# Layer 1 of a feed-forward block as Strassen block products, its weights streamed from scratch memory

## The chip, the cores and the metric

The kernel runs on one core of a Trainium2 chip. The metric is the device time of the whole program in microseconds. A core has five engines that run side by side and wait for one another through semaphores: TensorE (PE; its weight loads are shown as PEld), VectorE (DVE), ScalarE (ACT), GpSimd (POOL) and SyncE (SP), which here issues the transfers. PSUM is the memory that matmuls write; SBUF holds everything else on chip.

## The reference

For each of four batches a channel attention gives `x`, and a two-layer block follows:

```
qn = q / (norm of q over the tokens + 1e-6);  kn likewise            # [6080, 256]
s  = kn^T @ qn / tau                                                 # [256, 256]
a  = softmax of s over its last axis
x  = v @ a                                                           # [6080, 256]
h  = x @ w_in                                                        # [6080, 2048]
out = (max(h, 0) ** 2) @ w_out                                       # [6080, 256]
```

All inputs are float32, but the weights `w_in` (256 x 2048) and `w_out` (2048 x 256), which arrive as 64-bit floats and are decoded on chip. Four batches of 6080 tokens make 24320 rows.

## The kernel before

**Products in three terms.** Every float32 operand x of a large product is split into hi (x rounded to 12 significant bits) and lo = x - hi. A product is hi*hi + hi*lo + lo*hi, three matmuls that add up in one PSUM bank. ACT writes hi, DVE subtracts for lo.

**Folding.** (v a) w_in is computed as v (a w_in). For each batch, `fold` multiplies the softmax with a piece of `w_in` and leaves it in SBUF as the split pair `wph`, `wpl`, in four pieces of 512 feed-forward columns.

**Layer 1 and layer 2.** A batch is cut into 12 chunks of tokens, eleven of 512 and one of 448. A unit is one chunk and one tile of 128 feed-forward columns, so a chunk has 16 units. `layer1` (L287) does six matmuls into a bank `h` (two halves of the 256 channels, three terms each). ACT takes the Relu out of PSUM (`r`, L303) and squares it into `gh` (L306), DVE squares into `g` (L305) and subtracts for `gl` (L310). `layer2` (L316) follows two units later (`LAG`): six matmuls with the weights `woh` and `wol` into two banks `o`, which collect over the chunk's 16 units. Then ACT and DVE copy one bank each into `res`, which SP sends off.

**Side work.** Between the units of batch b the scores of batch b+1 are done: `score_load` (1 MB a load, four slots `kqt`), `score_norm` (ACT squares, DVE adds to `acc`), `score_split` (hi on ACT, lo on DVE), `score_mm` (six matmuls a tile of 128 rows, all 48 tiles into one bank of their own). After them follow the softmax (`norms`, `spread`, `exps`, `attnT`) and the folds for the next batch. `v` is loaded and split a chunk ahead (`load_v`, `split_v`).

**The start.** The first batch's scores come first, unsplit, while ACT and DVE take the norms; twelve tiles of the second batch follow as fill. The weights' 64-bit words are decoded by `decode_f64` (L65: four DVE and two ACT steps), piece by piece, the later ones among the units of the first two chunks, which share their pieces.

**Order.** Each step has a place in a list (`at(u, fn, ...)`: after unit u). Engines, slots and semaphores are the framework's: when the program is built, it arranges each engine's instructions by their place in the source and by when they are ready, so that an engine's order can differ from the source's. At run time each engine takes its instructions strictly in that built order.

Of the kernel before, what the change touches and what calls it, by code (L numbers as in the profile page):

```python
# [20 lines left out]
def tile_channel_attention_relu2_ffn(ctx, tc, kq, vT, tau, w_in, w_out, outT):  # L21
    """softmax over channels of normalised k^T q, then relu(x W_in)^2 W_out.

    Every float32 operand x of a large product is split exactly into hi = x rounded
    to 12 significant bits and lo = x - hi (float32r holds both), and
    hi*hi + lo*hi + hi*lo is accumulated in float32.  (v a) W_in is computed as
    v (a W_in).
    """
# [26 lines left out]
    win = const.tile([P, NH, DFF], F32, name="win")  # L55
    woh = const.tile([P, NJ, C], F32R, name="woh")
    wol = const.tile([P, NJ, C], F32R, name="wol")

    def h_bank():
        return ps_h.tile([P, CHUNK], F32, name="h", tag="h")  # L60

# [1 line left out]
    raws = {}  # L63

    def decode_f64(raw, W):  # L65
        """float64 words (low half first) to float32, rounded to nearest."""
        top = 122879.9921875
        shape = list(raw.shape[:3])
        hw = work.tile(shape, F32, name="hl", tag="hl", bufs=3)
        mag = work.tile(shape, F32, name="hl", tag="hl", bufs=3)  # L70
        low = work.tile(shape, I32, name="low", bufs=1)
# [10 lines left out]
    wiv = w_in.bitcast(U32).rearrange("(h p) f -> p h f", p=P)  # L82
    wov = w_out.bitcast(U32).rearrange("(j p) e -> p j e", p=P)

    def load_w_in(fc):
        raws["in", fc] = []
        for h, t in enumerate(("wph", "wpl")):
            raw = wpp.tile([P, FC, 2], U32, name=t, tag=t)
            nc.sync.dma_start(out=raw.rearrange("p n two -> p (n two)"),
                              in_=wiv[:, h, 2 * fc * FC:2 * (fc + 1) * FC])  # L90
            raws["in", fc].append(raw)

    def decode_w_in(fc):
        for h, raw in enumerate(raws.pop(("in", fc))):
            decode_f64(raw[:, None], win[:, h:h + 1, fc * FC:(fc + 1) * FC])

    def load_w_out(s):
        raw = work.tile([P, FPC, C, 2], U32, name="kqt", tag="kqt", bufs=KB)
        nc.sync.dma_start(out=raw.rearrange("p j n two -> p j (n two)"),
                          in_=wov[:, s * FPC:(s + 1) * FPC, :])  # L100
        raws["out", s] = raw

    def decode_w_out(s):
        js = slice(s * FPC, (s + 1) * FPC)
        W = work.tile([P, FPC, C], F32, name="sq", tag="sq")
        decode_f64(raws.pop(("out", s)), W)
        nc.scalar.copy(out=woh[:, js], in_=W)
        nc.vector.tensor_sub(out=wol[:, js], in0=W, in1=woh[:, js])  # L108

# [1 line left out]
    s_ps = {}  # L111
# [22 lines left out]
    def score_split(b, kt):  # L134
        x = kqt[b, kt // G][:, kt % G, :]
        hl = work.tile([P, 2, C2], F32R, name="hl", tag="hl", bufs=3)
        nc.scalar.copy(out=hl[:, 0], in_=x)  # L137
        nc.vector.tensor_sub(out=hl[:, 1], in0=x, in1=hl[:, 0])  # L138
        split[b, kt] = hl

    def score_mm(b, kt):
        if kt == 0:
            s_ps[b] = ps_s.tile([P, NH, C], F32, name="s")
        x = kqt[b, kt // G][:, kt % G, :]
        hl = split.pop((b, kt), None)
        for h in range(NH):
# [5 lines left out]
            for n, (l, r) in enumerate(terms):  # L152
                nc.tensor.matmul(out=s_ps[b][:, h, :], lhsT=l, rhs=r, start=kt == 0 and h == 0 and n == 0,  # L153
                                 stop=kt == NT - 1 and n == len(terms) - 1, skip_group_check=True)

# [34 lines left out]
    def spread(b):  # L190
        """the q norms' reciprocals, along the free axis of every partition."""
# [7 lines left out]
    def exps(b):  # L199
# [3 lines left out]
        for h in range(NH):  # L203
            e = small.tile([P, C], F32, name="e", bufs=2)
            nc.vector.scalar_tensor_tensor(out=e, in0=s_ps[b][:, h, :], scalar=z[:, h:h + 1],
# [23 lines left out]
    wp = {}  # L229
    wi = {}  # L230

    def fold_split(b, fc):
        wi[b, fc] = []
        for d in range(NH):
            w = work.tile([P, 2, FC], F32R, name="hl", tag="hl", bufs=3)
            x = win[:, d, fc * FC:(fc + 1) * FC]
            (nc.vector.tensor_copy if b else nc.scalar.copy)(out=w[:, 0], in_=x)
            nc.vector.tensor_sub(out=w[:, 1], in0=x, in1=w[:, 0])
            wi[b, fc].append(w)

    def fold(b, fc, ch):
# [21 lines left out]
    for b in range(B):  # L263
        for n0 in range(0, N, CHUNK):
            chunks.append((b, n0, min(CHUNK, N - n0)))
# [211 lines left out]
```

## Time and profile before

| | |
|---|---|
| runs of the kernel | 2286.97, 2287.17 and 2288.32 us; median 2287.17 us |
| the profiled execution, first to last instruction | 2286.2 us |
| matmuls in it | 10496 |

A profile is one execution. The page gives each engine's busy time and share of the span, the span in 40 slices (busy tenths, and GB/s that the transfers moved), and the chain of work that ended last, followed back from the last instruction. Then come groups of instructions: line, engine, operation, what is written and read with its shape, count, total busy time and mean duration in ns, and behind the second bar the idle time of the engine ahead of them with what ended it. A view by windows has, for each stretch, its length and then busy time and count of PE, PEld, DVE, ACT and POOL, the granted TensorE clock, the transfers' share and GB/s. A view in order of time gives start and length of each instruction in us. The row of a matmul is longer than the distance to the next, since matmuls overlap; their pace is read from starts.

### The profile page before, as it was taken

Reading aid. Unit: us, or ns where it says so; the run is one execution under the profiler, and the core shown is the slowest. Engines: PE = TensorE matmul, PEld = TensorE weight load, DVE = VectorE, ACT = ScalarE, POOL = GpSimd, SP = SyncE. Lnnn points to the kernel's source line nnn. Section 1 sums busy time; section 2 is a strip of 40 time slices with the busy share of each in tenths; the row PEclk is TensorE's granted clock in tenths of the full one; section 3 lists DMA queues with packets and bytes.
Section 4 is the critical chain, followed back from the end, with each engine's and each line's share of the span. In section 5 each row is a group of like instructions: output and inputs, shape, how many; then the busy total and the mean of one; then the engine's idle time right before and its main releaser. Section 6 shows DMA issues by size and latency. Waiting matters only on the chain.

```text
span 2286.2 us, 27309 instructions
## 1 busy us (share of the span) xinstructions
PE 2276.8 (100%) x10496; PEld 1913.3 (84%) x10496; DVE 1415.6 (62%) x2097; ACT 1246.0 (55%) x2033; POOL 0.8 (0%) x7
## 2 busy tenths in 40 slices
PE   9999999999999999999999999999999999999999
PEld 7788888888888888888888888888888888888888
DVE  7886656557656666655765666665566555555554
ACT  6885555546555555554654555555454445444444
POOL 0000000000000000000000000000000000000000
PEclk9999999999999999999999999999999999999999
DMA  9411111110011111111001111210001000000000
GB/s 350 156 56 56 37 38 65 47 42 32 19 36 56 56 37 56 55 56 55 19 20 53 37 56 38 74 37 19 18 19 36 19 19 29 28 19 24 31 10 18
DMA packets 37763, 110.29 MB, mean 48 GB/s; under 512 B 3456, under 2 KB 5504, under 8 KB 31616
## 3 DMA queue, kind: packets, MB, share of 16 engines
q1 hardware_dynamic: 37632, 108.54, 13.7%
q8 instruction: 82, 1.34, 0.2%
q14 instruction: 49, 0.40, 0.1%
HBM read 83.62 MB, written 24.90 MB: 47 GB/s over the span
## 4 chain that ended last, share of the span: by engine, by line
PE 98%; DMA 1%; DVE 1%; ACT 0%; issue 0%; SPq 0%; DVEq 0%
PE o L325 45%; PE h L296 45%; PE s L153 5%; PE h L253 2%; DMA kqt<-kq 1%; DMA v<-vT 0%; DVE acc L132 0%; PE h L169 0%; ACT sq L131 0%; DVE vl L282 0%; DVE low L78 0%; SPq L120 0%; PE h L220 0%; PE h L194 0%; ACT L175 0%
## 5 line engine op out<-in xcount | busy, mean ns | idle before, releaser
L305 DVE TENSOR_TENSOR g<-r 128x512 f32<-128x512 f32 (+1 forms) x752 | 515.9, 686 | 660.8 <-ACT r L303 660.4
L303 ACT ACTIVATE r<-h 128x512 f32<-128x512 f32 (+1 forms) x768 | 455.5, 593 | 860.2 <-PE h L296 856.0
L296 PE MATMUL h<-vh,wph 128*128 128x512 f32 (+1 forms) x1536 | 597.7, 389 | 0.0
L296 PE MATMUL h<-vl,wph 128*128 128x512 f32 (+1 forms) x1536 | 596.3, 388 | 0.0
L325 PE MATMUL o<-gh,woh 128*128 128x512 f32 (+1 forms) x1536 | 594.8, 387 | 0.8 <-ACT gh L309 0.8
L325 PE MATMUL o<-gl,woh 128*128 128x512 f32 (+1 forms) x1536 | 594.6, 387 | 0.5 <-DVE gl L310 0.5
L296 PE MATMUL h<-vh,wpl 128*128 128x512 f32 (+1 forms) x1536 | 594.7, 387 | 0.0
L325 PE MATMUL o<-gh,wol 128*128 128x512 f32 (+1 forms) x1536 | 594.6, 387 | 0.0
L310 DVE TENSOR_TENSOR gl<-g,gh 128x512 fp32r<-128x512 f32 (+1 forms) x768 | 527.0, 686 | 90.5 <-ACT gh L309 6.3
L306 ACT ACTIVATE gh<-r 128x512 fp32r<-128x512 f32 (+1 forms) x752 | 472.4, 628 | 21.6
L325 PEld LDWEIGHTS o<-gh,woh 128*128 128x128 f32 x1536 | 288.3, 188 | 58.6 <-ACT gh L309 1.3
L296 PEld LDWEIGHTS h<-vh,wpl 128*128 128x128 f32 x1536 | 288.4, 188 | 58.3 <-DVE wpl L258 0.4
L325 PEld LDWEIGHTS o<-gl,woh 128*128 128x128 f32 x1536 | 288.2, 188 | 58.1 <-DVE gl L310 1.2
L325 PEld LDWEIGHTS o<-gh,wol 128*128 128x128 f32 x1536 | 288.3, 188 | 57.1 <-DVE wol L108 0.3
L296 PEld LDWEIGHTS h<-vh,wph 128*128 128x128 f32 x1536 | 288.9, 188 | 53.3 <-DVE wpl L258 0.2
L296 PEld LDWEIGHTS h<-vl,wph 128*128 128x128 f32 x1536 | 288.9, 188 | 52.3
L132 DVE TENSOR_TENSOR acc<-acc,sq 128x1024 f32<-128x1024 f32 x92 | 112.4, 1222 | 29.5 <-ACT sq L131 26.1
L137 ACT CAST hl<-kqt 128x512 fp32r<-128x512 f32 x132 | 81.7, 619 | 77.1 <-PE s L153 75.3
L138 DVE TENSOR_TENSOR hl<-kqt,hl 128x512 fp32r<-128x512 f32 x132 | 91.1, 690 | 51.7 <-ACT hl L137 51.7
L153 PEld LDWEIGHTS s<-hl 128*128 128x128 f32 x792 | 112.4, 190 | 10.3
L153 PE MATMUL s<-hl 128*128 128x256 f32 x792 | 115.6, 282 | 0.0
L131 ACT ACTIVATE sq<-kqt 128x1024 f32<-128x1024 f32 x92 | 96.4, 1055 | 25.4 <-DMA kqt<-kq 21.0
(69 smaller groups left out, 614.3 us busy)
## 6 DMA issues: line engine op xcount, KB each, us to landing
kqt<-kq SPq DMA_DIRECT2D x47, 1024.0 KB, 4.8
v<-vT SPq DMA_DIRECT2D x44, 512.0 KB, 3.7
outT<-res SPq DMA_DIRECT2D x88, 256.0 KB, 2.0
kqt<-w_out SPq DMA_DIRECT2D x4, 1024.0 KB, 9.6
wph<-w_in SPq DMA_DIRECT2D x4, 512.0 KB, 9.4
wpl<-w_in SPq DMA_DIRECT2D x4, 512.0 KB, 10.0
v<-vT SPq DMA_DIRECT2D x4, 448.0 KB, 3.5
outT<-res SPq DMA_DIRECT2D x8, 224.0 KB, 1.9
```

Of the source, the lines that this page charges most:

```text
L131: nc.scalar.activation(out=sq, in_=x, func=AF.Square)
L132: nc.vector.tensor_add(out=accs[b], in0=accs[b], in1=sq)
L137: nc.scalar.copy(out=hl[:, 0], in_=x)
L138: nc.vector.tensor_sub(out=hl[:, 1], in0=x, in1=hl[:, 0])
L153: nc.tensor.matmul(out=s_ps[b][:, h, :], lhsT=l, rhs=r, start=kt == 0 and h == 0 and n == 0, stop=kt == NT - 1 and n == len(terms) - 1, sk ...
L253: nc.tensor.matmul(out=ps, lhsT=l[:, d, cs], rhs=wi[b, fc][d][:, r, :], start=n == 0, stop=n == 3 * NH - 1)
L296: nc.tensor.matmul(out=ps[:, :T], lhsT=l[:, ch, cs], rhs=r[:, ch, :T], start=n == 0, stop=n == 3 * NH - 1)
L303: nc.scalar.activation(out=r[:, :T], in_=ps[:, :T], func=AF.Relu)
L305: nc.vector.tensor_mul(out=g[:, :T], in0=r[:, :T], in1=r[:, :T])
L306: nc.scalar.activation(out=gh[:, :T], in_=r[:, :T], func=AF.Square)
L310: nc.vector.tensor_sub(out=gl[:, :T], in0=g[:, :T], in1=gh[:, :T])
L325: nc.tensor.matmul(out=o[:, :T], lhsT=l[:, j, es], rhs=r[:, :T], start=j == 0 and n == 0, stop=j == NJ - 1 and n == 2)
```

## The change

**Seven products for eight.** Two feed-forward tiles (f = 1, 2; tile j and tile j + 8) and two halves of a chunk of up to 1024 tokens (n = 1, 2) make a quad. Its layer 1 is a product of 2 x 2 blocks (the channels' halves are the inner blocks), and Strassen's scheme in Winograd's form takes seven block products of three terms for eight. `A11, A12, A22, S2, S3, S1, S4` are the weights' blocks and combinations. A batch has six chunks, five with halves of 512 tokens and one with halves of 480, and eight quads a chunk: 192 quads in all.

**The seven products** (m1 to m7) end in four blocks "11", "21", "22", "12". TensorE adds to a bank that already holds a sum, so some sums are copied by ACT from bank to bank (m1's from B to X, then S2's is added to B and copied to Z); m7 is copied to SBUF, and DVE adds it to B and Z out of PSUM (`plus_m7`). Each of the two banks `h` is used for B and m7 in turn, and for score pairs and folds. X and Z have one bank each, and layer 2 has four.

**The weights.** `combine` makes S1 to S4 from the folded weights, splits all seven and writes them to scratch memory in DRAM (128 x 2 x 7 x 128 words of 4 bytes, 917,504 bytes for one j). `load_wt` brings them back for every quad of every chunk but the first, into three slots. The decoded `w_in` goes to scratch too and is loaded again for each batch.

**Who does what.** The subtractions for the low parts of score tiles, of v's combinations (from the second chunk on) and of the later batches' weights move to or are added on POOL, as are the combinations themselves; for the first batch and the first chunk they run on DVE. Scores are gathered in pairs of tiles in an `h` bank and added to `s_acc` in SBUF by DVE (`score_burst`, `score_add`); score loads are 0.5 MB. At the start, the first piece of `w_in` is decoded behind the scores, `decode_w_out` stands ahead of the first quad, and the three later groups are prepared during the first chunk.

```diff
-    def layer1(ci, j):
...
-        for ch in range(NH):
-            for l, r in ((wh, vh), (wh, vl), (wl, vh)):
-                nc.tensor.matmul(out=ps[:, :T], lhsT=l[:, ch, cs], rhs=r[:, ch, :T],
...
+    def combine(b, g):
+        eng = nc.gpsimd if b else nc.vector
+        u = us.pop((b, g))
+        S = work.tile([P, 4, GW], F32, name="sq", tag="sq")
+        s2, s3, s1, s4 = (S[:, i] for i in range(4))
+        eng.tensor_add(out=s1, in0=u[:, 0, 1], in1=u[:, 1, 1])
+        eng.tensor_sub(out=s2, in0=s1, in1=u[:, 0, 0])
+        eng.tensor_sub(out=s3, in0=u[:, 0, 0], in1=u[:, 0, 1])
+        eng.tensor_sub(out=s4, in0=u[:, 1, 0], in1=s2)
+        for i in range(2):
+            j = 2 * g + i
+            w = work.tile([P, 2, NP, P], F32R, name="wt" if b == 0 else "wc", bufs=WB if b == 0 else 1)
+            js = slice(i * P, (i + 1) * P)
+            for o, x in ((w[:, :, 0:2], u[:, :, 0, js]), (w[:, :, 2:3], u[:, 1:2, 1, js]), (w[:, :, 3:7], S[:, :, js])):
+                nc.scalar.copy(out=o[:, 0], in_=x)
+                eng.tensor_sub(out=o[:, 1], in0=x, in1=o[:, 0])
+            wsc[b, j] = scratch.tile([P, 2, NP, P], F32, name=f"wsc{j}", bufs=2)
+            nc.sync.dma_start(out=wsc[b, j], in_=w.bitcast(F32))
...
+    def load_wt(ci, j):
+        wt[ci, j] = work.tile([P, 2, NP, P], F32R, name="wt", bufs=WB)
+        nc.sync.dma_start(out=wt[ci, j].bitcast(F32), in_=wsc[chunks[ci][0], j])
...
+    def v_combos(ci):
+        eng = nc.gpsimd if ci else nc.vector
...
+        t1 = diff(b12, b11)
+        t2 = diff(b22, t1)
+        for i, x in ((A11, lambda: b11), (S2, lambda: t2), (A12, lambda: b21), (S3, lambda: diff(b22, b12)),
+                     (A22, lambda: diff(b21, t2)), (S1, lambda: t1), (S4, lambda: b22)):
+            yield ci, i, x
+    def v_split(ci, i, x):
...
+        nc.scalar.copy(out=t[:, 0, :T], in_=x)
+        (nc.gpsimd if ci else nc.vector).tensor_sub(out=t[:, 1, :T], in0=x, in1=t[:, 0, :T])
...
+    def product(q, i, out, start):
+        ci, j = q
+        T = chunks[ci][2]
+        w, v = wt[ci, j], vt[ci, i]
+        for n, (l, r) in enumerate(((0, 0), (0, 1), (1, 0))):
+            nc.tensor.matmul(out=out[:, :T], lhsT=w[:, l, i], rhs=v[:, r, :T], start=start and n == 0,
+                             stop=n == 2, skip_group_check=True)
...
+    def block(q, c, ps=None, s=None):
...
+        if ps is not None:
+            nc.scalar.activation(out=r[:, :T], in_=ps[:, :T], func=AF.Relu)
+            nc.scalar.activation(out=gh[:, :T], in_=r[:, :T], func=AF.Square)
             nc.vector.tensor_mul(out=g[:, :T], in0=r[:, :T], in1=r[:, :T])
         else:
+            nc.vector.scalar_tensor_tensor(out=g[:, :T], in0=s[:, :T], scalar=0.0, op0=ALU.max,
+                                           in1=s[:, :T], op1=ALU.mult)
             nc.scalar.copy(out=gh[:, :T], in_=g[:, :T])
         nc.vector.tensor_sub(out=gl[:, :T], in0=g[:, :T], in1=gh[:, :T])
...
+    def m1(q):
+        st["B"] = h_bank()
+        product(q, A11, st["B"], True)
+        st["X"] = ps_x.tile([P, HMAX], F32, name="x")
+        nc.scalar.copy(out=st["X"][:, :T], in_=st["B"][:, :T])
+    def m6(q):
+        product(q, S2, st["B"], False)
+        st["Z"] = ps_z.tile([P, HMAX], F32, name="z")
+        nc.scalar.copy(out=st["Z"][:, :T], in_=st["B"][:, :T])
+    def m2(q):
+        product(q, A12, state[q]["X"], False)
+        block(q, "11", ps=state[q]["X"])
+    def m7(q):
+        H = h_bank()
+        product(q, S3, H, True)
+        nc.scalar.copy(out=state[q]["m7"][:, :T], in_=H[:, :T])
+    def m4(q):
+        product(q, A22, state[q]["B"], False)
+        state[q]["21"] = plus_m7(q, state[q]["B"])
+    def m5(q):
+        product(q, S1, state[q]["Z"], False)
+        state[q]["22"] = plus_m7(q, state[q]["Z"])
+        block(q, "21", s=state[q]["21"])
+        block(q, "22", s=state[q]["22"])
+    def m3(q):
+        product(q, S4, state[q]["Z"], False)
+        block(q, "12", ps=state[q]["Z"])
...
+    plan = (m1, ("11", 0), ("11", 1), ("21", 0), m6, m2, ("21", 1), m7, ("22", 0), m4, m5, ("22", 1), ("12", 0),
+            ("12", 1), m3)
...
+    def score_burst(b, kts):
+        s = h_bank()
+        for kt in kts:
+            score_mm(b, kt, s, kt == kts[0], kt == kts[-1])
+        score_add(b, s)
...
-    G = 4
+    G = 2
     KB = 4
-    EARLY = 3
+    HB = 3
+    TB = 3
+    WB = 3
+    VB = 8
+    GB = 5
+    EARLY = 6
...
+    decode_w_in(0)
+    early_mm(early[:4])
+    spread(0)
+    exps(0, s0)
+    fold_split(0, 0)
+    early_mm(early[4:8])
+    attnT(0)
+    for step in v_combos(0):
+        v_split(*step)
+    load_v(1)
+    early_mm(early[8:])
+    score_add(1, s1)
+    fold(0, 0, 0, ps_z.tile([P, HMAX], F32, name="z"))
+    fold(0, 0, 1)
+    decode_w_out(0, 0)
+    decode_w_out(0, 1)
+    combine(0, 0)
```

In `plan`, a name is a step of layer 1 of the current quad, and a pair ("21", 0) the three matmuls of layer 2 for that block of the quad before and one half of the output channels. Each step and each pair is three matmuls, 45 in a quad. `at(n - 1.5, load_wt, ci, j)` asks for a quad's weights one and a half quads ahead; `combine` of the next batch stands in the last seven quads of a batch, 1.4 quads apart.

More of the change, by code (lines that the diff above doesn't have):

```diff
@@ L80, in decode_f64 @@
                                        op0=ALU.bitwise_and, in1=low.bitcast(U32), op1=ALU.bitwise_or)
[L82 to L108, printed above, removed]
@@ L111, in tile_channel_attention_relu2_ffn, with load_w_in @@
-    s_ps = {}
+    wiv = w_in.bitcast(U32).rearrange("(h p) (t f) -> p h t f", p=P, t=2)
+    wov = w_out.bitcast(U32).rearrange("(t g j p) e -> p g t j e", p=P, t=2, j=2)
+    win = {}
+    def load_w_in(g):
+        raws["in", g] = []
+        for h in range(NH):
+            raw = work.tile([P, 2, GW, 2], U32, name="kqt", tag="kqt", bufs=KB)
+            nc.sync.dma_start(out=raw.rearrange("p t n two -> p t (n two)"),
+                              in_=wiv[:, h, :, 2 * g * GW:2 * (g + 1) * GW])
+            raws["in", g].append(raw)
@@ L269, in load_v @@
+    def load_wt(ci, j):
+        wt[ci, j] = work.tile([P, 2, NP, P], F32R, name="wt", bufs=WB)
+        nc.sync.dma_start(out=wt[ci, j].bitcast(F32), in_=wsc[chunks[ci][0], j])
+    widths = [min(HMAX, (N - n0) // 2) for n0 in range(0, N, 2 * HMAX)]
+    assert sum(widths) * 2 == N and all(w % 2 == 0 for w in widths)
+    chunks = [(b, 2 * sum(widths[:i]), w) for b in range(B) for i, w in enumerate(widths)]
+    NCH = len(widths)
+    raw_v = {}
+    vt = {}
     def load_v(ci):
         b, n0, T = chunks[ci]
-        v = work.tile([P, NH, CHUNK], F32, name="v", bufs=1)
@@ new lines, in plus_m7 @@
+    def plus_m7(q, ps):
+        T = chunks[q[0]][2]
+        s = work.tile([P, HMAX], F32, name="s", bufs=2)
+        nc.vector.tensor_add(out=s[:, :T], in0=ps[:, :T], in1=state[q]["m7"][:, :T])
+        return s
+    def m4(q):
[6 more added lines that the diff above has]
+        block(q, "22", s=state[q]["22"])
@@ new lines, in layer2 @@
+        o = outs[n, e]
+        wg, wj = j // 2, 2 * f + j % 2
+        es = slice(e * P, (e + 1) * P)
+        for k, (l, r) in enumerate(((woh, gh), (wol, gh), (woh, gl))):
+            nc.tensor.matmul(out=o[:, :T], lhsT=l[:, wg, wj, es], rhs=r[:, :T],
+                             start=first and k == 0, stop=last and k == 2)
+        if last:
+            res = work.tile([P, HMAX], F32, name="res", bufs=3)
+            (nc.vector.tensor_copy if e else nc.scalar.copy)(out=res[:, :T], in_=o[:, :T])
+            nc.sync.dma_start(out=ov[:, e, b * N + n0 + n * T:b * N + n0 + (n + 1) * T], in_=res[:, :T])
@@ L427, in tile_channel_attention_relu2_ffn @@
[L427 to L448 removed]
+        pairs = list(range(k0, NT, 2))
@@ new lines, in tile_channel_attention_relu2_ffn @@
+        end = when[pairs[-1]]
+        at(end + 0.6, score_burst, b, [NT - 2, NT - 1])
+        at(end + 0.8, norms, b)
+        at(end + 1.2, spread, b)
+        at(end + 1.3, lambda b=b: exps(b, s_acc[b]))
+        at(end + 1.9, attnT, b)
+        for g in range(NG):
+            u = u0 + QB - NJ + 1.0 + 1.4 * g
+            at(u - 1.5, load_win, b, g)
+            at(u - 0.3, fold_split, b, g)
+            at(u, fold, b, g, 0)
+            at(u + 0.4, fold, b, g, 1)
+            at(u + 0.5, combine, b, g)
@@ new lines, in tile_channel_attention_relu2_ffn, with start, run_side @@
+    for n, (ci, j) in enumerate(quads):
+        if ci:
+            at(n - 1.5, load_wt, ci, j)
+        if j == 0 and ci:
+            if ci > 1:
+                at(n - NJ + 2.05, load_v, ci)
+            def start(ci=ci, n=n):
+                for k, step in enumerate(v_combos(ci)):
+                    at(n + (-1.2, -0.95, -0.9, -0.6, -0.5, -0.4, -0.25)[k], v_split, *step)
+            at(n - 2.0, start)
+    def run_side(t):
+        while True:
+            due = sorted(u for u in side if u <= t)
+            if not due:
+                return
+            u = due[0]
+            todo = side.pop(u)
+            for fn, args in todo:
+                fn(*args)
```

350 lines of the change are left out of this document (172 added, 178 removed).

## The prediction

> **What bounds the kernel now.** I read the page's shares of the span and the transfer rates of its 40 slices first, then the chain that ended last, then the matmuls in order of time.
>
> ```profile
> span 2286.2 us, 27309 instructions
> ...
> PE 2276.8 (100%) x10496; PEld 1913.3 (84%) x10496; DVE 1415.6 (62%) x2097; ACT 1246.0 (55%) x2033; POOL 0.8 (0%) x7
> ...
> GB/s 350 156 56 56 37 38 65 47 42 32 19 36 56 56 37 56 55 56 55 19 20 53 37 56 38 74 37 19 18 19 36 19 19 29 28 19 24 31 10 18
> ...
> PE 98%; DMA 1%; DVE 1%; ACT 0%; issue 0%; SPq 0%; DVEq 0%
> ```
>
> TensorE is busy over all of the span, and 98% of the chain that ended last is TensorE. A busy share alone could hide pauses, because a row of a matmul is longer than its step; so I take the step from the starts of equal instructions twelve matmuls apart, for both chunk widths:
>
> ```profile
> 1899.75 0.39 PE L325 MATMUL o<-gh,wol 128*128 128x512 f32 x1
> 1902.47 0.39 PE L325 MATMUL o<-gh,wol 128*128 128x512 f32 x1
> ...
> 2259.65 0.36 PE L325 MATMUL o<-gh,wol 128*128 128x448 f32 x1
> 2262.08 0.36 PE L325 MATMUL o<-gh,wol 128*128 128x448 f32 x1
> ```
>
> At 512 columns twelve take 2.72 us, 0.2267 us each; at 448 they take 2.43 us, 0.2025 each. Twelve is exactly one unit (six of layer 1, six of layer 2), so in this stage nothing but the number of matmuls counts. 704 units of 2.72 and 64 of 2.43 us are 2070 us of the 2286: a change pays here if it removes matmuls and lets nothing else end last.
>
> **The matmuls removed.** Four units (two feed-forward tiles, two halves) have 24 matmuls of layer 1; seven products of three have 21. Layer 2 keeps its 24, so a quad has 45 matmuls for 48. The new chunks are five of 512 and one of 480 per batch and half, 8 quads each: 160 quads of 512, 32 of 480. Between the two measured steps, 480 columns take 0.2146 us. 160 x 45 x 0.2267 + 32 x 45 x 0.2146 = 1632 + 309 = 1941 us. **This removes 129 us.** Score, fold and early-score matmuls keep their numbers.
>
> **What the other engines get.** Their durations, one shape a row:
>
> ```profile
> L310 DVE TENSOR_TENSOR gl<-g,gh 128x512 fp32r<-128x512 f32 x704 | 487.0, 692 | 82.3 <-ACT gh L309 6.3 <-PE o L325 1.5 <-ACT gh L306 0.9
> L306 ACT ACTIVATE gh<-r 128x512 fp32r<-128x512 f32 x688 | 435.4, 633 | 19.6
> L303 ACT ACTIVATE r<-h 128x512 f32<-128x512 f32 x704 | 420.6, 597 | 801.2 <-PE h L296 799.7 <-DVE gl L310 1.5
> L132 DVE TENSOR_TENSOR acc<-acc,sq 128x1024 f32<-128x1024 f32 x92 | 112.4, 1222 | 29.5 <-ACT sq L131 26.1 <-ACT acc L128 0.5
> L131 ACT ACTIVATE sq<-kqt 128x1024 f32<-128x1024 f32 x92 | 96.4, 1055 | 25.4 <-DMA kqt<-kq 21.0 <-DVE acc L132 4.2
> L137 ACT CAST hl<-kqt 128x512 fp32r<-128x512 f32 x132 | 81.7, 619 | 77.1 <-PE s L153 75.3 <-PE h L253 1.5 <-DVE low L78 0.3
> L282 DVE TENSOR_TENSOR vl<-v,vh 128x512 fp32r<-128x512 f32 x88 | 60.2, 685 | 0.3 <-ACT vh L281 0.3
> L329 DVE COPY res<-o 128x512 f32<-128x512 f32 x44 | 30.1, 684 | 0.0
> L329 ACT COPY res<-o 128x512 f32<-128x512 f32 x44 | 25.1, 570 | 0.0
> masks.py:199 POOL TENSOR_SCALAR_AFFINE_SELECT ident<-ident 128x128 f32<-128x128 f32 x1 | 0.3, 294 | 0.0
> ```
>
> Per quad ACT does three copies out of PSUM (0.57), two Relu (0.60), two squares (0.63) and two casts (0.62): 5.4 us. DVE does two additions of m7, four g and four gl: ten of 0.69, 6.9 us. A quad takes TensorE 10.2 us, so both fit. About 0.65 score pairs fall on each quad of the score stage. A pair costs DVE 1.22 for the norm and 0.68 for the new addition out of PSUM, since scores now leave their bank after every pair, and ACT 1.06 + 2 x 0.62. That makes DVE 8.2 and ACT 7.0 us a quad. The pair's 12 matmuls widen the quad too. Their step comes from two rows of the chain, three units and one score tile of six matmuls apart:
>
> ```profile
> 872.04 1.39 PE h L296 x6
> 880.94 1.39 PE h L296 x6
> ```
>
> 8.90 - 3 x 2.72 = 0.74 us for six, so 0.65 x 1.48 = 1.0 us: 11.2 us a quad with scores.
>
> POOL, which does seven small things in the kernel before, gets the low parts of the score tiles, all of v's combinations from the second chunk on, and the later batches' weight combinations. Before has no POOL operation with two inputs. Below, I bound one of 512 elements by DVE's 0.69; above, by four times POOL's own row of 128 elements, 1.18. I take 1.18, the same engine. Per batch that is 48 + 66 + 8 subtractions of 512, 144 us, and about 26 us in `combine`: 170 us beside a TensorE stage of 531 us (40 quads of 10.2, eight of 9.66, 24 pairs of 1.48, 48 fold matmuls). POOL alone is no bound.
>
> **Steady waits.** A quad has new hand-overs: the copy X lies between m1 and m2, 12 matmuls or 2.72 us apart; Z likewise. From the end of m4 to the start of m3 there are also 2.72 us, in which DVE reads both banks, 2 x 0.69; 1.3 us are spare. A norm addition of 1.22 in front just fits; with the score addition too, m3 is 0.6 us late. A pair also takes one of the two `h` banks for its 1.48 us and the 0.68 of the addition; from m7's copy to the next m7 one is free for some 38 matmuls, 8.6 us, so that I cost at nothing. m3's lateness, over 66 pairs, is 40 us if it always happens and nothing if never. The order on an engine isn't the source's: the cast of v, written after the softmax, ran at 52.20, ahead of zq's copy:
>
> ```profile
> 52.20 1.12 ACT L281 CAST vh<-v 128x512 fp32r<-128x512 f32 x2
> ...
> 53.23 0.36 ACT L196 COPY zq<-h 128x256 f32<-128x256 f32 x1
> ```
>
> So work that isn't ready lets other work pass when the program is built, and I take less than half, **plus 22 us** with the folds' evictions. `combine` with its one `wc` buffer makes the second copies on ACT wait for POOL and a DMA; by the same ordering I cost that at nothing (18 us, 12 times 1.5, if a Z copy is stuck behind it).
>
> **The start.** Here the cover goes.
>
> ```profile
> 45.31 0.69 DVE L166 TENSOR_TENSOR acc<-acc 128x512 f32<-128x512 f32 x1
> ...
> 61.37 0.50 PE L296 MATMUL h<-vh,wph 128*128 128x512 f32 x1
> ...
> 64.47 3.18 PE L153 MATMUL s<-kqt 128*128 128x256 f32 x14
> ```
>
> ```profile
> L238 DVE TENSOR_TENSOR hl<-win,hl 128x512 fp32r<-128x512 f32 x32 | 22.0, 688 | 0.5
> L78 DVE CUSTOM_DVE_ANT_0 low<-hl,low 128x1024 uint16<-128x1024 uint16 x8 | 5.5, 687 | 0.6 <-ACT low L75 0.4
> L79 DVE SCALAR_TENSOR_TENSOR win<-hl,low 128x512 uint32<-128x512 uint32 x8 | 5.5, 685 | 0.0
> L205 DVE SCALAR_TENSOR_TENSOR e<-s,z,zq 128x256 f32<-128x256 f32 x8 | 3.7, 478 | 0.1
> L77 DVE TENSOR_SCALAR hl<-hl 128x512 int32<-128x512 int32 x8 | 3.4, 421 | 0.0
> L72 DVE TENSOR_SCALAR hl<-wph 128x512 f32<-128x512 f32 x4 | 1.7, 426 | 0.9 <-PE h L253 0.9
> ```
>
> Before, layer 1 begins at 61.4 with 3.2 us of early scores still to come. Afterwards DVE must do ahead of the first product, from about 45.3 us on: decoding the first w_in and w_out pieces (four halves of 0.43 + 0.42 + 0.69 + 0.69, 8.9), v's first chunk (four differences, seven low parts: 7.5), five norm additions (6.1), the softmax (about 5: the 0.69 of L166, two of 0.48, and small steps that I estimate at 3), the fold's low parts and aTl (2.1), the score copy (0.7) and combine up to its first tile (four of 0.45 and three of 0.3 to 0.7, about 3.2). That is 33 us, to about 78. The score loads, now of 0.5 MB with four in flight, cost nothing: by the last row above, 14 early matmuls take 3.2 us, so the eight of one load take 1.8, and three other loads cover 5.4 us (a load of twice the size landed in 4.8, quoted below); if they don't, some 3 us come on top. TensorE's own work there would end near 67. I take 77: **plus 12 us** against 64.6 (3 to 17).
>
> In the first chunk, weights are prepared for three more groups. Before, that stage had DVE at 87% and ACT at 86% (85.3 and 84.3 of 98.6 us), TensorE at 97.3 us, its clock granted in full (1.00):
>
> ```profile
> 61.37:160.00 98.63, 97.33 (x425) 79.31 (x425) 85.34 (x123) 84.34 (x135) 0.00 (x0) 1.00 0.27 95
> ```
>
> Now TensorE needs 8 x 10.2 + 36 fold matmuls = 90 us; DVE 8 x 6.9 + 3 x (8.9 decode, 1.4, 4.6 combine) + 1.4 = 101 us, and the steps hang on each other and on loads. I take **plus 16 us** (11 from the sums, 30 if v's and w_out's 17 POOL operations hold DVE up).
>
> **Streamed weights.** 184 loads and 32 stores of 0.92 MB, 198 MB, are 90 GB/s over the span. The slices above carry 10 to 156 after the first, which ran at 350.
>
> ```profile
> kqt<-kq SPq DMA_DIRECT2D x47, 1024.0 KB, 4.8
> ```
>
> A slightly larger load landed in 4.8 us; the weights are asked for 1.5 quads, 15 us, ahead. Cost: nothing, while SP isn't held by a full `kqt` ring.
>
> **Sum**, against the profiled execution: 2286.2 - 129 + 12 + 16 + 22 = 2207. The runs' median lies 1.0 us above that span: **2208 us**.
>
> **The rivals.** 1. **DVE and POOL don't run side by side.** Seven POOL operations at the start can't show this. If a POOL subtraction and a DVE operation with two inputs in SBUF exclude each other, what decides is DVE plus POOL per stage: 331 (quads) + 29 + 16 + 17 (norms, score additions, rest) + 170 = 563 us beside TensorE's 531, worst in the eight fold quads, where combine piles up. Never overlapping, three batches lose 32 us each: 2208 + 96 = 2304, slower than before. It needs 84 of those 96 us to be slower by over 0.2%; DVE's reads of PSUM and its idle time should hide a part, so half, 2256, is this rival's own middle. For it: at 1.18 us DVE and POOL exceed the stage. Against it: at 0.69 POOL shrinks to about 100 us, and the sum to 493. The Trainium skill, "SBUF — State Buffer", section "Who interferes with whom", says that a DVE instruction with two SBUF inputs contends with a GpSimd instruction that reads SBUF, and elsewhere on that page that the loser blocks for the whole instruction; by that rule this rival holds in full, and no run here shows it yet.
> 2. **TensorE waits at the hand-overs in every quad with scores**, 0.6 us or more on 109 quads, and combine blocks ACT: 2186 + 65 + 18 = 2269. For it: one X and one Z bank. Against: the spare 1.3 us.
> 3. **Everything is hidden**: no steady wait, the start at its lower bounds: 2286 - 129 + 3 + 11 + 1 = 2172.
> 4. **The weights come late** behind blocked loads on SP, 0.5 us a quad: 2208 + 92 = 2300. Against it: the 15 us of lead.
>
> **How the numbers follow.** Forecast 0.55 (2178 to 2235), rival 1 0.25 (0.09 of it slower, 0.03 the same), rival 2 0.10, rival 3 0.06, rival 4 0.04 (half slower). Faster 0.85, same 0.04, slower 0.11; 0.2%, 4.6 us, is about what a measurement tells from no change. From 2178 to 2292 about 0.17 is left out.
>
> **What would show it.** Right: 4032 layer-1 matmuls of unchanged step; the first product near 77 us; the second chunk begun near 182; TensorE's busy time short of the span by some 50 us, most of it before 190. Rival 1: DVE rows of 128x512 clearly above 692 ns wherever POOL is busy, and TensorE gaps released by DVE in the last eight quads of a batch. Rival 2: gaps ahead of m2, m3 and m5 released by ACT or DVE at unchanged durations. Rival 4: gaps released by DMA. The forecast fails if POOL's subtraction is far from 1.18 us, or if the start runs past 200 us.

## The result and the profile after

| | us |
|---|---|
| before, 4 runs | 2286.62 to 2288.32, median 2287.07 |
| after, 4 runs | 2416.30 to 2426.01, median 2421.07 |
| ratio | 1.0585, 95% interval 1.057 to 1.060 |
| the profiled execution after, span | 2419.3 |

The changed kernel is 134 us slower where the prediction had it 79 us faster; 2421 lies outside its range. The page after, first its shares:

```profile
span 2419.3 us, 27297 instructions
...
PE 2243.9 (93%) x9920; PEld 1827.8 (76%) x9920; DVE 1696.8 (70%) x2343; ACT 1361.5 (56%) x2389; POOL 722.7 (30%) x544
...
wt<-wsc SPq DMA_DIRECT2D x184, 896.0 KB, 4.6
```

The matmuls that were to go are gone, 10496 - 9920 = 576, and the streamed weights land in 4.6 us. But TensorE, busy for all of the span before, now has 175 us in which it does nothing, and POOL went from 0.8 to 723 us. Where the pauses lie is seen in the first chunk of the last batch, which has no side work beside it. The view by windows (length, then busy time and count of PE, PEld, DVE, ACT and POOL, granted clock, transfers' share, GB/s), first for the chunk's first quad, then for its other seven:

```profile
1895.60:1911.40 15.80, 11.94 (x46) 9.32 (x45) 9.76 (x12) 7.51 (x15) 10.74 (x7) 0.89 0.43 156
1911.40:1982.80 71.40, 71.40 (x316) 59.14 (x315) 47.92 (x72) 39.02 (x68) 6.23 (x6) 1.00 0.29 97
```

Seven quads take 10.20 us each with TensorE busy throughout, exactly the predicted pace. The first takes 15.8, and in it POOL works for 10.7 us: on the last three low parts of this chunk's `v` and, once the next `v` has landed, on the first four operations for that. The clock granted in it is 0.89: behind TensorE's pause of 3.31 us three matmuls take 1.45 us from start to start, where three took 0.70 ahead of it, so the pause costs speed after it as well. So it goes at every chunk between the first and the last: by the starts of their first products, first quads take 12.7 to 20.6 us, where a quad takes 10.2, or 11.7 with a score pair. The last chunk's first quad takes 10.3; no `v` follows it, and POOL works for 4.3 us in it.

The groups by shape show the second sign. DVE and POOL after:

```profile
L387 DVE TENSOR_TENSOR gl<-g,gh 128x512 fp32r<-128x512 f32 x640 | 493.7, 790 | 74.6 <-ACT gh L386 21.9 <-ACT gh L381 12.8 <-ACT x L396 0.5
L382 DVE TENSOR_TENSOR g<-r 128x512 f32<-128x512 f32 x320 | 268.4, 839 | 313.2 <-ACT r L380 309.1
L419 DVE TENSOR_TENSOR s<-h,m 128x512 f32<-128x512 f32 x160 | 110.0, 687 | 66.4 <-PE h L369 53.9 <-ACT m L414 12.3 <-issue 0.2
L150 POOL TENSOR_TENSOR hl<-kqt,hl 128x512 fp32r<-128x512 f32 x132 | 184.0, 1413 | 718.1 <-ACT hl L149 703.0 <-DVE gl L387 14.9
L357 POOL TENSOR_TENSOR vt<-tt,vt 128x512 fp32r<-128x512 f32 x76 | 124.8, 1653 | 369.7 <-ACT vt L356 369.5
```

DVE's operations with two inputs in SBUF take 790 and 839 ns on average (692 before), the addition that reads PSUM on one side (L419) takes 687, as it does without POOL in experiment 3, and POOL needs 1.41 to 1.65 us for what I had taken at 1.18. One boundary in order of time (start, length, instruction, in brackets the idle time before it and what ended it):

```profile
1985.67 1.74 POOL L357 TENSOR_TENSOR vt<-v,vt 128x512 fp32r<-128x512 f32 x1
1986.18 1.78 DVE L382 TENSOR_TENSOR g<-r 128x512 f32<-128x512 f32 x1
...
1987.44 0.33 SPq L328 DMA_DIRECT2D v<-vT  x1
...
1991.29 0.62 ACT L356 CAST vt<-v 128x512 fp32r<-128x512 f32 x1 [5.29 <-DMA v<-vT]
...
1992.29 0.59 ACT L403 COPY z<-h 128x512 f32<-128x512 f32 x1
...
1992.93 0.98 PE L369 MATMUL h<-vt,wt 128*128 128x512 f32 x3 [3.19 <-ACT z L403]
```

POOL's last low part ends at 1987.41, and only then can `v`, which has one buffer, be loaded again. ACT's first cast of the next `v` waits for that load, and the copy of Z, which TensorE waits for, stands behind the cast in ACT's order. TensorE's largest waits in the whole kernel (us in total, times, longest) are these:

```profile
PE h L369 <- ACT x L396: 51.5, 34, 6.7
PE h L369 <- ACT z L403: 51.0, 21, 3.5
PE z L369 <- DVE s L419: 18.8, 18, 3.0
PE o L454 <- DVE gl L387: 14.9, 20, 3.2
```

By these, 102 us end with ACT's copies of X and Z and 34 us with DVE. So two explanations offer themselves: an **order** on ACT that makes TensorE wait for a load (and, more generally, a chain POOL, load, ACT, TensorE), and the **ports**: DVE and POOL hold each other up, rival 1 of the prediction. The experiments are to part them.

### The profile page after: what moved, and what is told of

The parts are those of the page before. It is cut to its first block, busy times and chain, and to the rows that moved or that the text cites. A ratio compares the mean times of both kernels' runs of the same rounds, so it can differ in the third digit from the quotient of the medians.

```text
span 2419.3 us, 27297 instructions
## 1 busy us (share of the span) xinstructions
PE 2243.9 (93%) x9920; PEld 1827.8 (76%) x9920; DVE 1696.8 (70%) x2343; ACT 1361.5 (56%) x2389; POOL 722.7 (30%) x544
## 5 line engine op out<-in xcount | busy, mean ns | idle before, releaser
L369 PE MATMUL h<-vt,wt 128*128 128x512 f32 (+1 forms) x2304 | 668.2, 399 | 112.4 <-ACT x L396 51.5
L369 PEld LDWEIGHTS h<-vt,wt 128*128 128x128 f32 x2304 | 431.3, 191 | 229.7 <-ACT x L396 69.9
L382 DVE TENSOR_TENSOR g<-r 128x512 f32<-128x512 f32 (+1 forms) x384 | 323.0, 841 | 398.7 <-ACT r L380 394.0
L386 ACT CAST gh<-g 128x512 fp32r<-128x512 f32 (+1 forms) x384 | 230.7, 615 | 349.1 <-DVE g L384 348.8
L150 POOL TENSOR_TENSOR hl<-kqt,hl 128x512 fp32r<-128x512 f32 x132 | 184.0, 1413 | 718.1 <-ACT hl L149 703.0
L369 PE MATMUL z<-vt,wt 128*128 128x512 f32 (+1 forms) x1152 | 334.6, 399 | 19.0 <-DVE s L419 18.8
L384 DVE SCALAR_TENSOR_TENSOR g<-s 128x512 f32<-128x512 f32 (+1 forms) x384 | 289.1, 791 | 0.3
L369 PEld LDWEIGHTS z<-vt,wt 128*128 128x128 f32 x1152 | 218.1, 192 | 72.6 <-DVE s L419 29.5
L381 ACT ACTIVATE gh<-r 128x512 fp32r<-128x512 f32 (+1 forms) x384 | 240.9, 627 | 8.8
L419 DVE TENSOR_TENSOR s<-h,m 128x512 f32<-128x512 f32 (+1 forms) x192 | 130.9, 682 | 80.7 <-PE h L369 61.0
L369 PE MATMUL x<-vt,wt 128*128 128x512 f32 (+1 forms) x576 | 167.7, 399 | 0.0
```

Source lines behind the costliest of these rows:

```text
L150: nc.gpsimd.tensor_sub(out=hl[:, 1], in0=x, in1=hl[:, 0])
L369: nc.tensor.matmul(out=out[:, :T], lhsT=w[:, l, i], rhs=v[:, r, :T], start=start and n == 0, stop=n == 2, skip_group_check=True)
L381: nc.scalar.activation(out=gh[:, :T], in_=r[:, :T], func=AF.Square)
L382: nc.vector.tensor_mul(out=g[:, :T], in0=r[:, :T], in1=r[:, :T])
L384: nc.vector.scalar_tensor_tensor(out=g[:, :T], in0=s[:, :T], scalar=0.0, op0=ALU.max, in1=s[:, :T], op1=ALU.mult)
L386: nc.scalar.copy(out=gh[:, :T], in_=g[:, :T])
```

## The experiments

The kernel before took 2287.5 to 2288.0 us (medians) beside them. A time without a range is that of a single run; four and five runs of one kernel lay within 10 us for the changed kernel and some 3 for those of experiments 3 and 10. Edits are against the changed kernel unless another is named.

**1. The cast alone.** The first cast of the next chunk is placed behind m7's copy.

```diff
+        if ci and i == A11:
+            with tc.issue_after(behind["m7"]):
+                nc.scalar.copy(out=t[:, 0, :T], in_=x)
```

> The first cast of the next chunk's v (the one that finds a free slot) is placed on ACT behind the m7 copy of two quads before the chunk, and nothing else. Theory 'order': in the changed kernel ACT stands at that cast until v's load lands, 23 times 4.4 us, and the Z copy behind it holds TensorE; the first quad of a chunk without scores should fall from 15.9 us to 10.2 to 11, and the whole by 23 x 5.5 = 127 us to about 2295 us. Theory 'ports' (DVE and POOL exclude each other and that is the loss): no change, 2405 to 2430 us.

2380.27 us: 41 less, between the two. In the last batch, first quads fall from between 14.8 and 16.1 to 10.9 us, but in four of five chunks the second quads rise from 10.2 or 10.7 to between 12.7 and 14.6. Much of the stall moves and doesn't go.

**2. The same, and `combine`'s high parts on POOL**, so that no copy of ACT stands behind POOL's sums there.

```diff
-                nc.scalar.copy(out=o[:, 0], in_=x)
+                (nc.gpsimd.tensor_copy if b else nc.scalar.copy)(out=o[:, 0], in_=x)
```

> As the run before, and the high parts of the later batches' weight combinations are written by POOL in place of ACT, so that ACT has nothing to wait for in combine (35 us for POOL's sums, 28 us for the one wc buffer's transfer). Theory 'order': the last chunk of the first three batches falls from 111 to 115 us to about 98, some 15 us each, 45 in all: about 2250 us. Theory 'ports': POOL gets 72 more operations, and DVE is held up more: 5 to 30 us slower than the run before.

2393.44 us (ratio to before 1.0464, 1.0445 to 1.0483), 13 more than the kernel of experiment 1: more work on POOL, more time. 'Order' fails here.

**3. No arithmetic on POOL.** All of its subtractions and additions go to DVE, six lines of this kind:

```diff
-        (nc.gpsimd if ci else nc.vector).tensor_sub(out=t[:, 1, :T], in0=x, in1=t[:, 0, :T])
+        nc.vector.tensor_sub(out=t[:, 1, :T], in0=x, in1=t[:, 0, :T])
```

> Every POOL subtraction and addition is done by DVE instead; the order of the source and all buffers stay. Theory 'ports': DVE's two-input operations return from 0.80 to 0.69 us, POOL's waits go, and the time falls by 60 us or more. Theory 'order': the cast of v still stands ahead of the Z copy, so the first quads stay near 15 us; DVE gets some 330 us more and gives back about 110, stands near 1920 us of busy time, and the whole stays within 40 us of 2421.

One run gave 2197.42 us. Then five more runs of the same kernel:

> The kernel without POOL arithmetic again, timed. By its first look 2197 us, a ratio of 0.960 to 0.962 to the kernel before.

2200.33 us (2198.46 to 2201.54), ratio 0.9616, interval 0.9603 to 0.9629. The page of the single run, shares of the span and the chain that ended last:

```profile
span 2195.3 us, 27067 instructions
...
PE 2163.9 (99%) x9920; PEld 1800.7 (82%) x9920; DVE 1767.4 (81%) x2880; ACT 1365.3 (62%) x2389; POOL 0.8 (0%) x7
...
PE 91%; DMA 3%; DVE 3%; ACT 1%; issue 1%; SPq 0%; ACTq 0%; DVEq 0%
```

DVE does 537 operations more than after, and yet its busy time grows by 71 us only (1767.4 against 1696.8). Their groups say why; two rows of this kernel:

```profile
L387 DVE TENSOR_TENSOR gl<-g,gh 128x512 fp32r<-128x512 f32 x640 | 428.9, 688 | 39.1 <-ACT gh L381 4.2 <-ACT gh L386 2.3
L382 DVE TENSOR_TENSOR g<-r 128x512 f32<-128x512 f32 x320 | 220.0, 688 | 165.1 <-ACT r L380 160.9
```

Without POOL beside it DVE is back at 688 ns. The Strassen change itself is worth about what was forecast, 87 us for 79; the work on POOL costs 2421 - 2200 = 221 us. Not all of that is pauses: of the 224 us between the two profiles, 144 are more idle time of TensorE and 80 are more busy time for the same 9920 matmuls, part of it the ends of rows that no next matmul overlaps, part a lower granted clock (0.974 in place of 0.997 over the span).

**4. The ports by themselves.** A kernel that computes nothing of the reference runs 24 operations of 128x512 on each of two engines, alone and side by side.

```python
for ops in ((dve_two,), (pool_two,), (dve_two, pool_two), (dve_psum,), (dve_psum, pool_two), (dve_copy,),
            (dve_copy, pool_two), (act_one, pool_two)):
    for i in range(N):
        for op in ops:
            op(i)
    tc.strict_bb_all_engine_barrier()
```

> Computes nothing of the reference: 24 operations of 128x512 at a time, DVE with two SBUF inputs, POOL with two SBUF inputs, both at once, then DVE with one input from PSUM, DVE copies and ACT copies beside POOL. If DVE and POOL exclude each other for whole operations, the rows of both rise to the sum of the two alone (0.69 + about 1.2 = 1.9 us) when both run, and DVE with an input from PSUM stays at 0.68. If they don't, 0.69 and about 1.2 stay. From the rows of the changed kernel (DVE 0.79 to 0.84, POOL 1.3 to 1.65) I expect something of the first.

Its timeline, each row one run of equal operations (L37: DVE, two inputs in SBUF; L41: DVE, one input in PSUM; L45: DVE's copy; L49: POOL, two inputs; L53: ACT's cast):

```profile
4.41 14.53 DVE L37 TENSOR_TENSOR dtwo<-a,b 128x512 f32<-128x512 f32 x24
19.12 29.32 POOL L49 TENSOR_TENSOR ptwo<-c,d 128x512 fp32r<-128x512 f32 x24 [18.68 <-SPq L60]
48.59 39.03 DVE L37 TENSOR_TENSOR dtwo<-a,b 128x512 f32<-128x512 f32 x24 [29.65 <-SPq L60]
48.62 40.12 POOL L49 TENSOR_TENSOR ptwo<-c,d 128x512 fp32r<-128x512 f32 x24 [0.19 <-SPq L60]
88.89 29.03 DVE L41 TENSOR_TENSOR dpsum<-p,b 128x512 f32<-128x512 f32 x48 [1.27 <-SPq L60]
103.52 29.37 POOL L49 TENSOR_TENSOR ptwo<-c,d 128x512 fp32r<-128x512 f32 x24 [14.78 <-SPq L60]
132.96 40.92 DVE L45 COPY dcopy<-a 128x512 f32<-128x512 f32 x48 [15.05 <-SPq L60]
141.29 33.71 POOL L49 TENSOR_TENSOR ptwo<-c,d 128x512 fp32r<-128x512 f32 x24 [8.40 <-SPq L60]
175.18 29.38 POOL L49 TENSOR_TENSOR ptwo<-c,d 128x512 fp32r<-128x512 f32 x24 [0.19 <-SPq L60]
```

POOL alone takes 29.32 / 24 = 1.22 us each, close to the 1.18 of the prediction. DVE alone takes 14.53 / 24 = 0.61 from one to the next (a row of one is longer, 0.69, because successive ones overlap). Side by side POOL takes 40.12 / 24 = 1.67 and DVE 39.03 / 24 = 1.63. Strict turns would be 14.5 + 29.3 = 43.9 us, no contention 29.3; measured were 40.1. DVE with one input in PSUM (48 in 29.03 us, 0.60 each, half of them beside POOL) and ACT's casts leave POOL at 29.4. The Trainium skill, "SBUF — State Buffer", section "Who interferes with whom", has DVE with two SBUF inputs contend with a GpSimd instruction that reads SBUF, and not with one SBUF input outside its two-port modes: this run agrees on which contend. Of the full block that the page states, 10.8 of 14.5 us show here.

**5. Which part of POOL's work costs what.** Three kernels as in experiment 3, each with one part back on POOL: `v` alone, the low parts of the score tiles alone, the weights alone (`combine`, the folds' and `w_out`'s low parts). Against experiment 3, the main lines of the three:

```diff
-        nc.vector.tensor_sub(out=t[:, 1, :T], in0=x, in1=t[:, 0, :T])
+        (nc.gpsimd if ci else nc.vector).tensor_sub(out=t[:, 1, :T], in0=x, in1=t[:, 0, :T])
...
-        nc.vector.tensor_sub(out=hl[:, 1], in0=x, in1=hl[:, 0])
+        nc.gpsimd.tensor_sub(out=hl[:, 1], in0=x, in1=hl[:, 0])
...
-        eng = nc.vector
+        eng = nc.gpsimd if b else nc.vector
```

> POOL does v's differences and low parts alone (253 operations); everything else that it had is done by DVE. Theory 'chunk end': what costs is that v's seven tiles and the next load hang on POOL's slow operations at the end of a chunk, with SP, ACT and then TensorE held behind them; the first quads stay at 15 to 16 us and the time is near 2197 + 23 x 5.6 = 2326 us, 2310 to 2360. Theory 'ports everywhere' (the loss goes with POOL's busy time, 390 of 722 us): 2197 + 0.54 x 224 = 2318 us, but spread over the quads in which POOL works. The two differ in the next run.

> POOL does the low parts of the score tiles alone (132 operations, 184 of its 722 us), beside DVE in 66 quads. Theory 'ports everywhere': 2197 + 0.25 x 224 = 2254 us. Theory 'chunk end': DVE's two-input rows rise and a score tile is late by a microsecond, but nothing waits for it within a quad: 2190 to 2210 us.

> POOL does the low parts of w_out, of the folds' w_in and the combinations of the later batches' weights alone (some 150 us). Theory 'chunk end', widened to the last chunk of a batch, where ACT's copies in combine wait for POOL's sums and for the wc buffer: 3 x 15 to 20 us and up to 12 us in the first chunk, 2240 to 2265 us. Theory 'ports everywhere': 2197 + 0.2 x 224 = 2243 us, so this run does not tell the two apart by its total; the chunks in which it lies do.

2348.51, 2231.51 and 2243.43 us: 148, 31 and 43 more than 2200.33, together 222 of the 221. The parts add up, as well as single runs can tell. Scores cost a little in each of many quads: POOL works on them for 186 us, spread thin. The weights' 43 us lie in the three chunks in which the next batch's are prepared, 12 to 16 us in each. Such a chunk with the weights on POOL, by windows:

```profile
540.10:643.90 103.80, 94.58 (x412) 77.38 (x411) 75.48 (x104) 62.69 (x121) 44.38 (x45) 0.98 0.56 198
```

and the same chunk without POOL (experiment 3):

```profile
536.40:627.90 91.50, 91.17 (x414) 76.86 (x413) 79.64 (x148) 63.02 (x121) 0.00 (x0) 1.00 0.63 224
```

`v` is the dear one, 148 / 23 = 6.4 us on average for the 23 chunks whose `v` POOL splits; the last of them, whose first quad has 4.2 us of POOL in it, loses next to nothing.

**6. Two buffers for `v`** (paid for with one of `res`), so that its load needn't wait for POOL: with `v` alone on POOL, and in the changed kernel.

```diff
-        v = work.tile([P, NH, 2, HMAX], F32, name="v", bufs=1)
+        v = work.tile([P, NH, 2, HMAX], F32, name="v", bufs=2)
...
-            res = work.tile([P, HMAX], F32, name="res", bufs=3)
+            res = work.tile([P, HMAX], F32, name="res", bufs=2)
```

> As the run with v alone on POOL (2348.5 us), with two slots for v's chunk in place of one (and two for res in place of three, for room): POOL does the same 253 operations beside DVE, but the next load no longer waits for the last of them. Theory 'chain' (POOL's last subtraction ends late, SP's load waits for it, the cast of the next chunk stands in front of the Z copy on ACT and the outputs' transfers behind the load on SP): first quads fall from 16 to 10.2 to 12 us, the whole to 2205 to 2250 us. Theory 'exclusion' (DVE is held up so long by POOL that its own results are late for TensorE): the first quads stay above 14 us, 2310 to 2360 us.

> The changed kernel with two slots for v's chunk (two for res) and nothing else. Theory 'chain': what v costs goes, what scores and weights on POOL cost (31 and 43 us in the runs alone) stays: 2421 - 148 = 2273 us, 2270 to 2310. Theory 'exclusion': 2390 to 2425 us.

2342.66 and 2433.81 us, 6 less and 13 more; 6 us between two single runs are no clear difference. That speaks against the chain, but the run isn't clean. The waits of the first of the two kernels (us in total, times, longest) have a new one:

```profile
ACT res L458 <- DMA outT<-res: 87.0, 18, 8.8
```

ACT's copy into `res` now waits for an earlier output's transfer, because a buffer of `res` was given away. I had moved the wait, not removed it.

**7. The chain without the new wait.** `v` in two half tiles out of three buffers, and `res` with three again (against `pool_v_only`).

```diff
-        v = work.tile([P, NH, 2, HMAX], F32, name="v", bufs=1)
+        v = [work.tile([P, 2, HMAX], F32, name="v", bufs=3) for h in range(NH)]
```

> v's split alone on GpSimd, as in pool_v_only (2348.5 us), but v in two half tiles out of three buffers, and three buffers of res as in the changed kernel. The next chunk's upper half has a buffer of its own, so neither its load nor ScalarE's first cast stands behind GpSimd's last operation, and unlike in pool_v_two_bufs no output waits for a buffer of res (there 8.4 us at one chunk's start). Theory 'chain through the load of v': the extra 5.7 us in the first quads of the chunks go, 2210 to 2260 us. Theory 'GpSimd is late' (11 operations of 1.2 to 1.7 us, 13 to 18 us, for parts that are wanted within one quad of 10.2 us, since only the eighth buffer of vt is free before): 2320 to 2350 us. Theory 'VectorE is held up at the chunk's end': 2320 to 2350 us too.

2320.6 us: 28 of the 148 go. 120 stay, with the load out of the way. The chain that ended last, by engine, had pointed at that load; in `pool_v_only`:

```profile
PE 73%; POOL 8%; DMA 7%; ACT 6%; DVE 4%; issue 2%; SPq 0%; POOLq 0%; DVEq 0%; ACTq 0%
```

and in this kernel:

```profile
PE 71%; DVE 12%; ACT 5%; POOL 4%; DMA 4%; issue 3%; SPq 0%; DVEq 0%; POOLq 0%; ACTq 0%
```

Such a chain names only what came last. With the load gone the time falls by a fifth of what `v` costs and DVE takes most of its place, so it must have been nearly as late before. TensorE's waits say the same. In `pool_v_only` the largest ended with ACT's copies of Z (28.2 us) and X (20.4), and `s` held it for 14.8. In this kernel they are:

```profile
PE z L369 <- DVE s L419: 48.6, 33, 3.5
PE o L454 <- DVE gl L387: 15.9, 16, 2.4
PE h L369 <- ACT x L396: 9.6, 15, 1.3
```

A boundary of this kernel by windows, the quad before it, the stretch of the boundary, and a quad after it:

```profile
2048.00:2058.20 10.20, 10.20 (x46) 8.45 (x45) 6.83 (x10) 6.63 (x12) 5.06 (x4) 1.00 0.25 90
2058.20:2073.40 15.20, 12.87 (x54) 9.79 (x53) 15.07 (x15) 8.54 (x16) 12.53 (x8) 1.00 0.32 105
...
2083.60:2093.80 10.20, 10.20 (x47) 8.45 (x46) 6.57 (x11) 5.33 (x9) 0.00 (x0) 1.00 0.26 90
```

While POOL works for 12.5 us, DVE is busy for 15.07 of 15.20 us with only 15 operations, 1.00 us each, where an undisturbed quad has eleven in 6.57, 0.60 each. DVE isn't the busiest engine of the kernel (78%), but for these 15 us it is full, and TensorE runs out of its results. The run alone doesn't tell whether DVE's delay or POOL's own lateness would be enough by itself; the next one does.

**8. The contention without any wait for POOL.** As in experiment 3, DVE does everything; POOL makes as many subtractions in the places of `v`'s split, into a tile that nothing reads.

```diff
+        if ci:
+            for _ in range(2 if i in (S2, S3, A22, S1) else 1):
+                spare = work.tile([P, HMAX], F32, name="spare", bufs=1)
+                nc.gpsimd.tensor_sub(out=spare[:, :T], in0=t[:, 0, :T], in1=t[:, 0, :T])
```

> All arithmetic on VectorE as in np_no_pool (2200.3 us), and beside it 11 GpSimd subtractions per chunk after ScalarE's casts, at the places of v's split, into a tile that nothing reads. Nothing waits for GpSimd, so only what it takes from VectorE is left. Theory 'VectorE is held up': most of the 148 us come back, 2290 us or more. Theory 'GpSimd is late': 2205 to 2260 us, since VectorE's own parts of v lose some time as well.

2388.97 us, 189 more than 2200.33. POOL's results are thrown away, and TensorE and DVE never wait for it; ACT does for 4.3 us in all, three times, for a buffer of `vt` that POOL still reads. DVE's 2880 operations are the same as in experiment 3, but they keep it busy for 1939.5 us in place of 1767.4. The waits of this kernel, TensorE's largest:

```profile
PEld z L373 <- DVE s L423: 71.1, 36, 3.8
...
PE z L373 <- DVE s L423: 57.3, 27, 3.4
...
PEld o L458 <- DVE gl L391: 50.9, 26, 2.9
PE o L458 <- DVE gl L391: 39.5, 21, 2.5
```

All of them are released by DVE: `s`, the addition that frees B and Z, and `gl`. The first of these reads PSUM and isn't slowed itself; it stands in DVE's order behind operations that are. So POOL's work that nobody needs is enough for a loss of this size, and 'GpSimd is late' falls as the main cause. That it costs more than 148 has a likely reason, too: DVE has `v`'s own parts to make at the same time, and they take 85 of the 174 us by which its rows are longer. For that reason the run doesn't measure how much of the 148 in `pool_v_only` is DVE held up.

**9. Less of it.** `v` on POOL, but its four differences per chunk on DVE (against `pool_v_only`).

```diff
-        eng = nc.gpsimd if ci else nc.vector
+        eng = nc.vector
```

> v's split as in pool_v_only, but its four differences per chunk on VectorE: GpSimd makes the seven low parts alone, 8.5 to 12 us of it per chunk at 1.2 to 1.7 us. Theory 'GpSimd is late': this fits about one quad of 10.2 us, so 2210 to 2250 us. Theory 'VectorE is held up', in proportion to GpSimd's time (7 of 11 operations of 148 us): 2290 to 2300 us.

2291.98 us, 92 more than 2200.33. Seven operations for eleven, 7 / 11 x 148 = 94: the cost goes with POOL's time, as the hold-up has it, and 'GpSimd is late' (10 to 50) misses again.

**10. The start.** Experiment 3, with the first `combine` ahead of `decode_w_out`.

```diff
+    combine(0, 0)
     decode_w_out(0, 0)
     decode_w_out(0, 1)
-    combine(0, 0)
```

> Without POOL arithmetic, and at the start combine stands ahead of the two pieces of w_out (eight DVE operations, 4.4 us, which layer 2 needs a quad later). If DVE sets the first product, as the prediction has it, that product comes 3 to 5 us earlier than 77 to 80 us and the whole is 2195 us; if layer 2 then waits for w_out, no gain: 2200 us.

2198.18 us (2196.90 to 2199.81), ratio 0.9608, interval 0.9594 to 0.9621. Its first product runs at 77.2 us; two runs of the kernel of experiment 3 had 77.4 and 80.0. The two kernels can't be told apart; both beat the kernel before by 3.9% and the changed one by 9%.

## Why the prediction was wrong

**The step that failed** is the cost of POOL's work. The sum has no term for it: the forecast took 170 us a batch "beside a TensorE stage of 531 us", and `combine` "at nothing". That work cost 221 us (experiment 3), because DVE and POOL hold each other up where POOL's work is dense. Rival 1 had the right mechanism but was mis-sized, in two ways.

*It averaged over a batch.* The rival set DVE plus POOL, 563 us, against 531, and lost 32 us a batch at most. But POOL's work comes in bursts, and what doesn't fit into the quads of a burst is lost there: TensorE, busy for 99% of the span without POOL's work, has no idle time later in which to get it back. From the numbers of experiments 3 and 4: a quad gives DVE ten operations, eight with two inputs in SBUF. Beside a busy POOL they take 8 x 1.63 + 2 x 0.61 = 14.3 us, and a quad is 10.2. Eleven operations of POOL for `v` last 11 x 1.67 = 18.4 us, 1.29 such quads, and each is 4.1 us too long: 5.3 us a chunk as an estimate, 6.4 measured for `v` alone. Over POOL's 722.7 us the same share, 4.1 / 14.3, would be 207 us; 221 were measured. That the two agree so well is partly luck, because the parts don't: 31 of 186 us for the scores, where a burst is short and the spare 3 us of a quad can take it up, and 148 of 394 for `v`, of which 28 are the chain through the load.

*It bounded the price by a sum.* Contention slows both sides, 0.61 to 1.63 and 1.22 to 1.67, so POOL's work takes longer and holds DVE longer. The 96 us were no upper bound, and half of them less so. That DVE's idle time would hide a part is right where work is thin, and wrong at the chunks' ends.

I had also named the wrong place: the last eight quads of a batch, where `combine` piles up, cost 43 us, while `v`, at the chunks' ends, costs 148 and was named for the first chunk only. Of rival 1's two signs the longer rows came; the gaps released by DVE came only in part, since in the changed kernel most of TensorE's waits end with ACT.

**The other steps**, read from the kernel without arithmetic on POOL, where nothing else covers them:

- *129 us of matmuls removed*: right. 9920 matmuls, quads of 10.20 us to the hundredth, also in the changed kernel.
- *Start plus 12*: right. The first product runs at 80.3 in the changed kernel and at 77.4 and 80.0 in two runs without POOL (77 was forecast).
- *First chunk plus 16*: right without POOL, where the second chunk begins at 180.4 and 182.9 (182 was forecast). DVE bounds this chunk, as the sums had it; I had 101 us of DVE. By windows, the changed kernel:

```profile
80.30:196.70 116.40, 97.62 (x372) 73.27 (x373) 112.03 (x180) 80.66 (x152) 38.85 (x20) 0.91 0.50 177
```

and the one without POOL, both from about the first product to the second chunk:

```profile
77.40:180.40 103.00, 91.63 (x373) 69.84 (x374) 99.51 (x191) 76.49 (x147) 0.00 (x0) 0.95 0.56 195
```

  DVE does eleven operations fewer in the first row and is busy 12.5 us longer. The larger of my two prices, 30 us "if v's and w_out's 17 POOL operations hold DVE up", named that case.
- *Steady waits plus 22*: too high by some 10 us. 2207 less 2195.3 is 12, and two of them are the start and first chunk's.
- *Streamed weights at nothing*: right. 4.6 us to land in both kernels, and TensorE waits for none; rival 4 is out.
- *POOL's 1.18 us*: right for POOL alone (1.22), wrong beside DVE (1.41 to 1.65 in the changed kernel).
- *The built order lets ready work pass*: half right. It put the cast that waits for `v` ahead of Z's copy, and `combine`'s high parts ahead of others, presumably because POOL's work is taken to be done sooner than it is when the program is built (no run shows the reason); in `v` alone the chain through the load is 28 of 148 us (experiment 7).

What stays open: how the other 120 us of `v` divide between DVE held up and POOL's own parts late (experiments 7 to 9 make the first the larger); how the 43 us of the weights divide between DVE held up and ACT waiting for POOL's sums (35.0 us of ACT's waits in the changed kernel, 11 times); and how much of the 41 us of experiment 1 is the chain through `v`'s load, which in experiment 7, with less on POOL, is 28.

## What to carry to other kernels

An engine with little to do isn't free if its work slows one that others wait for: look at what DVE does in the same microseconds, not at the busy shares of the span. Price contention in the stretch in which it happens (how much longer does the unit of work get, times how many units the burst lasts), because an engine that is busy for nearly the whole span has no time left to get a stall back. If an experiment takes a buffer from elsewhere, look in its waits for the one that it has made.

## What the runs showed of the hardware

- DVE (two inputs in SBUF) and POOL side by side take very nearly turns: a pair takes 1.63 to 1.67 us, and 0.61 + 1.22 = 1.83 one after the other. DVE, the faster one, loses most: 2.7 times its time against 1.4 times for POOL.
- DVE's plain copy of float32 in SBUF contends as well: beside 24 of POOL's subtractions 24 copies took 32.6 us in place of 8.1 alone, and POOL's 24 took 33.7 in place of 29.3.
- POOL's first subtraction of the changed kernel took 5.42 us, the same shape later 1.26. By the timeline:

```profile
83.05 5.42 POOL L120 TENSOR_TENSOR wol<-wo,woh 128x512 fp32r<-128x512 f32 x1 [81.64 <-ACT woh L119]
...
89.87 1.26 POOL L120 TENSOR_TENSOR wol<-wo,woh 128x512 fp32r<-128x512 f32 x1
```

It falls into the first chunk. In the other kernels with subtractions on POOL the first one took 2.6 to 8.2 us as well; in experiment 4, where it ran with DVE idle, it took 1.26 like those after it. So it isn't a price of every first use, and what it is was not tried.
